# A decode kernel's first load, 128 rows of wq, issued as sixteen rows and then 112, with the load behind it issued after the framework's barrier

## The chip, the cores and the metric

The kernel runs on one core of a Trainium2 chip. The metric is the device time of one execution in microseconds (us). The times of the kernel before are three runs: median 1362.75, from 1362.43 to 1364.05.

## The reference

One token goes through a block with attention over a cache and a gated feed-forward part, side by side, all in float32:

```python
xn = _layernorm(x)                                    # x: 1 x 1 x 576
q = (xn @ wq).reshape(B, Sq, H, Dh)                   # wq: 576 x 4096, 32 heads of 128
scores = einsum("bhqd,bhkd->bhqk", q, k_cache) * Dh ** -0.5   # k_cache: 32 heads x 16384 x 128
o = einsum("bhqk,bhkd->bhqd", softmax(scores), v_cache)       # v_cache: as k_cache
h = gelu(xn @ w_gate) * (xn @ w_up)                   # 576 x 4608 each
return x + o @ wo + h @ w_down                        # wo: 4096 x 576, w_down: 4608 x 576
```

The two caches are 268 MB each; all that the kernel has to read is 587.6 MB.

## The kernel before, in words

The program is written out by hand as one list of operations for each engine (class `Plan`). `Plan.op` and `Plan.dma` append to an engine's list with the semaphore counts that it has to wait for; `Plan.ahead` issues the first operations of a list before the framework's barrier, and `Plan.run` emits the rest behind it, in the block at L128. Nothing reorders the lists.

All large loads go out from SyncE (SP), in the order of its list, so they stand one behind the other in one DMA queue, which 16 DMA engines work off. Each load of 128 rows is 128 packets of one row each where a row is up to 64 KB (the cache's rows of 64 KB are one packet, and those of wq's first load are 32 KB). The order is:

- wq in three loads: `qw[0]` (128 partitions, 32 KB each, the first and second of four row groups), `qt` (the 64 tail rows of wq, laid on 128 partitions, 8 KB each), `qw[1]` (as `qw[0]`, the third and fourth row group);
- w_gate, and behind VectorE's work on wq w_up, in the same three parts;
- K and V of the heads in turn, 8.4 MB each, in a loop, each behind the release of its buffer (`s_kf` after VectorE's sums, `s_vf` after TensorE's use of V);
- w_down in two parts and wo in many, at the end.

The projections of the token are made on VectorE: `rows` multiplies the first row group by its part of the token (L264), adds the second (L253), then the tail's, then the third and fourth. Its first product waits for the load `qw[0]`, its third step for `qt`, its fourth for `qw[1]`. TensorE sums over the partitions behind it. In the loop VectorE makes K times q (L356) and the sums (L360); TensorE makes the product with V (L344). At the end VectorE adds the products of w_down and of a part of wo to `wacc` (L253), TensorE those of the rest of wo (L478), and 2.3 KB are written.

`Plan.ahead` is called with two operations of SP and one of ACT: the loads `qw[0]` and `qt` on SP and the token's row `xrow` on ACT stand before the barrier; all else is behind it.

Of the kernel before, what the change touches and what calls it, by code (L numbers as in the profile page):

```python
# [13 lines left out]
P = 128  # L14
# [8 lines left out]
HD = H * DH  # L23
# [9 lines left out]
SIDE = 160  # L33
LEFT = 2 * SIDE
ASIDE = 8
SEL = 396


class Plan:
# [14 lines left out]
    def op(self, e, fn, *deps, sig=None, by=1):  # L54
        if e in ("dve", "act", "pool"):
            deps += (self.last.get(e),)
        sig = sig or self.own[e]
        self.count[sig.name] = self.count.get(sig.name, 0) + by
        self.q[e].append((deps, fn, sig, by))
        if sig is self.own[e]:  # L60
            self.last[e] = sig, self.count[sig.name]
        return sig, self.count[sig.name]

    def dma(self, e, out, in_, *deps, sem=None):
        sem = sem or self.sem(f"d{len(self.count)}")
        return self.op(e, lambda g: g.dma_start(out, in_), *deps, sig=sem, by=16)
# [55 lines left out]
@with_exitstack  # L122
def kernel(ctx: ExitStack, tc: tile.TileContext, x, k_cache, v_cache, wq, wo, wg, wu, wd, out):
    pl = Plan(tc)
    last, done = plan(tc.nc, pl, x, k_cache, v_cache, wq, wo, wg, wu, wd, out)
    pl.ahead({"sp": 2, "act": 1})
    tc.close()
    tc.compile()  # L128
    pl.run(last, done)


def plan(nc, pl, x, k_cache, v_cache, wq, wo, wg, wu, wd, out):
    op, dma = pl.op, pl.dma
# [10 lines left out]
    def small(name, shape, where=None):  # L144
        if where is None:
            size = 4
            for n in shape[1:]:
                size *= n
            where = place[name] = top[0]
            top[0] += -(-size // 32) * 32  # L150
            assert top[0] <= S0, (name, top)
        return nc.alloc_sbuf_tensor_at(name, shape, F32, offset=where).ap()

    def big(name, floats, where):
        assert where + 4 * floats <= 3 * SLOT
        return nc.alloc_sbuf_tensor_at(name, [P, floats], F32, offset=S0 + where).ap()
# [14 lines left out]
    gu, hT = small("gu", [P, 2, FT]), small("hT", [P, FT])  # L171
    sel = small("tmp", [P, 3 * SEL])
    over = place["tmp"]
# [7 lines left out]
    qw, qt = [big("q0", 2 * HD, C + 8 * HD), big("q2", 2 * HD, C)], big("qt", HD // 2, C - 2 * HD)  # L181
    both = big("both", 12 * SEL, C + 8 * DF + 256)
    gw, gt = [big("g0", 2 * DF, B + 10240), big("g2", 2 * DF, A - 4 * DF)], big("gt", DF // 2, B)
# [21 lines left out]

    main = {n: w[:DM].rearrange("(p j) f -> p (j f)", j=DJ) for n, w in (("q", wq), ("g", wg), ("u", wu))}
    tail = {n: w[DM:].rearrange("d (s f) -> (d s) f", s=2) for n, w in (("q", wq), ("g", wg), ("u", wu))}
    d_q = [dma("sp", qw[0], main["q"][:, : 2 * HD]), dma("sp", qt, tail["q"]), dma("sp", qw[1], main["q"][:, 2 * HD :])]
    d_x = dma("act", xrow, xf)
    d_g = [dma("sp", gw[0], main["g"][:, : 2 * DF]), dma("sp", gt, tail["g"]), dma("sp", gw[1], main["g"][:, 2 * DF :])]  # L210

# [49 lines left out]
    def rows(w, t, d, parts, between=None):  # L261
        n = w[0].shape[-1] // 2
        r = [u[:, j * n : (j + 1) * n] for u in w for j in range(2)]
        op("dve", lambda g: g.tensor_scalar(r[0], r[0], xp[:, :1], None, op0=ALU.mult), d[0], k_x)  # L264
        add(r[1], r[1], xp[:, 1:2], r[0])
        made = between and between()
        for i in range(2):
            c = r[1][:, i * n // 2 : (i + 1) * n // 2]
            add(c, t, xt[:, i : i + 1], c, d[1])
        k_s = add(r[2], r[2], xp[:, 2:3], r[1], d[2])  # L270
        v = [u.rearrange("p (i c) -> p i c", i=4) for u in (r[3], r[2])]
        for lo, hi, to in parts:
            k = add(bv[:, :, to : to + hi - lo], v[0][:, :, lo:hi], xp[:, 3:4], v[1][:, :, lo:hi])
        pads = [op("pool", lambda g, lo=lo, hi=hi: g.memset(bv[:, :, lo:hi], 0.0), k_s)
                for lo, hi in ((384, SEL), (SEL + 384, 2 * SEL), (2 * SEL + 256, 3 * SEL)) if len(parts) > 1]
        pl.then("dve", [s_r], k, *pads[-1:])
        return k_s, k, made

    def sums(g):
        with g.Fori(0, 3):  # L280
# [3 lines left out]
            for b in range(3):  # L284
                for i in range(4):
                    m = g.matmul(pw[32 * i : 32 * i + 32, b, :SEL], ones[:, :32], bv[:, i, b * SEL : (b + 1) * SEL], start=True, stop=True)  # L286
            m.then_inc(s_w, 1)
# [3 lines left out]
    def select(dst, c, r, n):  # L291

        t = dst.shape[-1]
        v = sel[:, : 3 * c].rearrange("p (b r t) -> p b r t", b=3, t=t)
        m = m32[:, : 3 * c // t].rearrange("p (b r) -> p b r", b=3).unsqueeze(3).to_broadcast([P, 3, c // t, t])
        k = op("dve", lambda g: g.tensor_mul(v, pw[:, :, :c].rearrange("p b (r t) -> p b r t", t=t), m), (s_w, n), c_m32)
        return op("dve", lambda g: g.tensor_reduce(dst, sel[:, : r * t].rearrange("p (r t) -> p t r", r=r), axis=AX.X, op=ALU.add), k)  # L297

    _, q_k, _ = rows(qw, qt, d_q, [(384 * b, min(384 * b + 384, HD // 4), SEL * b) for b in range(3)])
    d_u = [dma("sp", uw[0], main["u"][:, : 2 * DF], q_k), dma("sp", ut, tail["u"]), dma("sp", uw[1], main["u"][:, 2 * DF :])]  # L300
# [8 lines left out]

    u_k, _, k_g = rows(uw, ut, d_u, [(0, DF // 4, 0)], lambda: select(gu[:, 0], SEL, 32, 2))  # L310

# [132 lines left out]
    for n in WO_CUTS:  # L444
        w, base, dep = (wo0, 0, (s_kf, 2)) if lo < WO1 else (wo1, WO1, k_w0)
        c = w[:, (lo - base) * D : (lo - base + n) * D]
        d = dma("sp", c, wov[:, lo * D : (lo + n) * D], dep)
# [22 lines left out]
    for t in ON_DVE:  # L470
        for i, c in enumerate((oT[: P // 2, WT - 1 :], o31) if t == ASIDE else ()):
            to = o_sum[: P // 2, LEFT:]
# [19 lines left out]
    for i, t in enumerate(rows):  # L492
        w, d = d_wo[t]
        k = whole(32 * (i % 4), oT[:, t : t + 1], w, (d, k_oT), i < 4, i >= len(rows) - 4)
    k_part = op("dve", lambda g: g.tensor_tensor(part, acc[:, :, :HALF], wacc, op=ALU.add), k, k_w1)  # L495
    for t in range(WT - LAST, WT - 2):
        w, d = d_wo[t]
# [14 lines left out]
    d = dma("sp", of, to, c, c0, c1)  # L512
# [28 lines left out]
```

## Time and profile before

| what | before |
|---|---|
| median of three runs | 1362.75 us (1362.43 to 1364.05) |
| profiled execution: span, first to last instruction | 1360.5 us |
| profiled execution: its own time, taken as the median | 1362.75 us, 2.25 us around the span |
| DMA: data read in the span, mean rate | 587.60 MB, 432 GB/s |
| DMA engines busy with the hardware queue of SP and ACT | 99.8% |
| VectorE (DVE) busy | 1243.5 us, 91% |
| TensorE (PE) busy | 391.3 us, 29% |

No time is listed for the profiled execution beside its span, so its own time is taken as the span and what lies around it. The span of 1360.5 us lies 2.25 us below the median of the three runs, and that difference stands for what lies ahead of the first instruction and behind the last one. In the tables by window, the DMA share is the packet time of the 16 DMA engines in the stretch, and a packet is counted whole in the stretch where it starts: so a short stretch in which 16 packets start can show a share over 1, and one in which none starts shows 0 although all engines are busy. Share times length is then the mean time of a packet, when 16 start in the stretch.

### The profile page before, as it was taken

To read this page: it belongs to the slowest core of one execution; us is meant where nothing else is said; L and a number is where in the kernel's file an instruction comes from. 1 tells how busy PE (TensorE), PEld (TensorE's weight loads), DVE (VectorE), ACT (ScalarE), POOL (GpSimd) and SP (SyncE) were. 2 spreads that over 40 slices of the span, in tenths; PEclk is the share of its full clock that TensorE was granted. 3 is DMA by queue.
4 is the path that set the end of the run, shared out by engine and by line. 5 is a ranking of instruction groups with operands and counts; after the bars stand their busy time and mean duration, and the time that the engine had idled before them with its cause. 6 is when DMAs were issued, how large, how long until landed. Compare 5 with 4: busy or idle time off the path is not lost. (4 is left out here: it accounts for less than half of the span.)

```text
span 1360.5 us, 6992 instructions
## 1 busy us (share of the span) xinstructions
PE 391.3 (29%) x2650; PEld 122.4 (9%) x2650; DVE 1243.5 (91%) x228; ACT 66.9 (5%) x234; POOL 36.0 (3%) x25
## 2 busy tenths in 40 slices
PE   0211233333211333333222333332223333322136
PEld 0000011001000111100000111010001111000011
DVE  7999999999988888898888888998888889988888
ACT  0000000000000000000000000000000000000000
POOL 0063000000000000000000000000000000000000
PEclk9655666666556666666556666655666666655667
DMA  9999999999999999999999999999999999999998
GB/s 405 429 437 432 434 447 441 432 432 432 434 432 434 432 432 432 435 451 435 432 432 432 434 432 434 432 432 432 441 447 434 432 432 434 432 434 432 431 432 374
DMA packets 12870, 587.63 MB, mean 432 GB/s; under 512 B 1474, under 2 KB 1986, under 8 KB 2756
## 3 DMA queue, kind: packets, MB, share of 16 engines
q1 hardware_dynamic: 12866, 587.60, 99.8%
q8 instruction: 1, 0.02, 0.0%
q10 hardware_dynamic: 2, 0.00, 0.0%
q14 instruction: 1, 0.01, 0.0%
HBM read 587.60 MB, written 0.00 MB: 432 GB/s over the span
## 5 line engine op out<-in xcount | busy, mean ns | idle before, releaser
L344 PE MATMUL po<-vt,pe 128*4 128x512 f32 x2048 | 291.8, 733 | 611.5 <-PEq L119 611.5
L356 DVE TENSOR_TENSOR kb<-kb,qb 128x16384 f32<-128x16384 f32 (+1 forms) x17 | 277.3, 16314 | 31.8 <-DVEq L119 31.8
L356 DVE TENSOR_TENSOR ka<-ka,qb 128x16384 f32<-128x16384 f32 x16 | 275.6, 17226 | 32.1 <-DVEq L119 32.1
L360 DVE TENSOR_REDUCE sc<-kb 128x128 f32<-128x16384 f32 x16 | 275.5, 17220 | 2.3
L360 DVE TENSOR_REDUCE sc<-ka 128x128 f32<-128x16384 f32 x16 | 275.5, 17220 | 2.3
L344 PEld LDWEIGHTS po<-vt,pe 128*4 128x4 f32 x2048 | 56.3, 98 | 819.9 <-issue 819.9
L337 PE MATMUL pt<-ident,pm 128*1 128x128 f32 x32 | 11.9, 372 | 223.1 <-PEq L119 223.1
L397 ACT ACTIVATE o<-po 128x512 f32<-128x512 f32 x32 | 19.1, 597 | 877.1 <-ACTq L119 877.1
L349 PE MATMUL pc<-m,o 128*128 128x1 f32 x256 | 32.7, 249 | 28.9 <-PEq L119 28.9
L349 PEld LDWEIGHTS pc<-m,o 128*128 128x128 f32 x256 | 31.0, 191 | 57.8 <-issue 57.8
L253 DVE SCALAR_TENSOR_TENSOR wacc<-wd,hT,wacc 128x576 f32<-128x576 f32 x36 | 29.5, 819 | 4.1 <-DMA wd<-in_B_w_down_dram 2.9
L286 PE MATMUL pw<-both,ones 128*32 128x396 f32 x72 | 11.5, 801 | 63.3 <-PEq L119 63.3
L365 DVE TENSOR_REDUCE nm<-pt 1x1 f32<-1x128 f32 x32 | 8.9, 278 | 21.5 <-DVEq L119 21.5
L337 PEld LDWEIGHTS pt<-ident,pm 128*1 128x1 f32 x32 | 2.5, 79 | 228.2 <-issue 228.2
L339 PE MATMUL pb<-nm,ones 1*128 1x1 f32 x64 | 17.7, 343 | 18.5 <-PEq L119 18.5
L339 PEld LDWEIGHTS pb<-nm,ones 1*128 1x128 f32 x64 | 15.9, 307 | 27.8 <-issue 27.8
L393 ACT ACTIVATE nb<-pb 128x1 f32<-128x1 f32 x32 | 5.5, 171 | 254.1 <-ACTq L119 254.1
L363 DVE TENSOR_REDUCE pm<-sc 128x1 f32<-128x128 f32 x32 | 9.2, 286 | 7.6 <-DVEq L119 7.6
L335 PE MATMUL pqb<-qsel,hsel 128*128 128x128 f32 x64 | 14.9, 315 | 1.8 <-PEq L119 1.8
L395 ACT ACTIVATE pe<-sc,nb 128x128 f32<-128x128 f32 x32 | 12.8, 401 | 6.1 <-ACTq L119 6.1
L304 ACT ACTIVATE hsel<-hcol 128x128 f32 (+1 forms) x34 | 10.2, 301 | 41.3 <-DVE qsel L297 41.2
L326 POOL TENSOR_TENSOR tmp<-tmp 128x576 f32<-128x576 f32 (+3 forms) x4 | 11.3, 2836 | 0.3
(93 smaller groups left out, 177.9 us busy)
## 6 DMA issues: line engine op xcount, KB each, us to landing
g<-in_B_w_gate_dram SPq DMA_DIRECT2D x2, 4608.0 KB, 39.5
u<-in_B_w_up_dram SPq DMA_DIRECT2D x2, 4608.0 KB, 32.3
q<-in_A_wq_dram SPq DMA_DIRECT2D x2, 4096.0 KB, 17.4
kb<-in_A_k_cache_dram SPq DMA_DIRECT2D x2, 4096.0 KB, 26.7
wd<-in_B_w_down_dram SPq DMA_DIRECT2D x1, 8064.0 KB, 42.0
wo<-in_A_wo_dram SPq DMA_DIRECT2D x1, 3456.0 KB, 35.9
wo<-in_A_wo_dram SPq DMA_DIRECT2D x2, 1728.0 KB, 28.6
wd<-in_B_w_down_dram SPq DMA_DIRECT2D x1, 2304.0 KB, 28.1
```

What stands on the lines that cost most here:

```text
L253: return op("dve", lambda g: g.scalar_tensor_tensor(out, w, c, into, op0=ALU.mult, op1=ALU.add), *deps)
L286: m = g.matmul(pw[32 * i : 32 * i + 32, b, :SEL], ones[:, :32], bv[:, i, b * SEL : (b + 1) * SEL], start=True, stop=True)
L326: k = op("pool", lambda g, o=o, r=r: g.tensor_tensor(o, v[:, :r, :], v[:, r : 2 * r, :], op=ALU.add), k)
L335: g.matmul(pqb[:, 0, :DH], hsel, qsel, start=True, stop=True).then_inc(s_pq, 1)
L337: g.transpose(pt[:1, 0, :P], pm, ident).then_inc(s_pt, 1)
L339: g.matmul(pb[:, 0, :1], ones[:1, :], nm, start=True, stop=True).then_inc(s_pb, 1)
L344: m = g.matmul(po[q : q + 4, 0, :], pe[:, k : k + 4], vt[:, k * DH : (k + 4) * DH], start=k < 16, stop=k >= N - 16)
L349: m = g.matmul(pc[:, 0, :1], o4[:, j * DH : (j + 1) * DH], m32[:, j : j + 1], start=j == 0, stop=j == 3)
L356: g.tensor_mul(kd, kd, qb[i].unsqueeze(1).to_broadcast([P, n[1] - n[0], DH])).then_inc(s_d, 1)
L360: g.tensor_reduce(sc[i], kt[i].rearrange("p (n d) -> p n d", d=DH), axis=AX.X, op=ALU.add).then_inc(s_d, 1)
L395: g.activation(pe, sc[i], AF.Exp, bias=nb, scale=SCALE, accum_out=ls[:, bass.ds(h, 1)]).then_inc(s_p, 1)
L397: g.activation(o4, po[:, 0, :], AF.Copy).then_inc(s_o4, 1)
```

## The change

The load of `qw[0]` is made as two loads: partitions 0 to 15, and partitions 16 to 127. Both count up one semaphore, `wq`, by 16 each, and VectorE's first product waits for its value 32, that is for both. `Plan.ahead` still takes two operations of SP, which are now these two; the load `qt` stands behind the barrier, ahead of `qw[1]`.

```diff
+FIRST = 16
...
-    d_q = [dma("sp", qw[0], main["q"][:, : 2 * HD]), dma("sp", qt, tail["q"]), dma("sp", qw[1], main["q"][:, 2 * HD :])]
+    s_q = pl.sem("wq")
+    for a, b in ((0, FIRST), (FIRST, P)):
+        d = dma("sp", qw[0][a:b], main["q"][a:b, : 2 * HD], sem=s_q)
+    d_q = [d, dma("sp", qt, tail["q"]), dma("sp", qw[1], main["q"][:, 2 * HD :])]
```

SP's list at the start of the program before. `q_98` is `qw[0]`, `q_99` is `qw[1]`, `g_102` and `gt` are parts of w_gate; the branch at L128 is the entry of the block, the wait ahead of L113 is the barrier.

```order
0 L536 UNCONDITIONAL_BRANCH [waits barrier_Pool_Activation_PE_DVE_SP_release]
1 L66 DMA q_98<-in_A_wq_dram 128x8192
2 L66 DMA qt<-in_A_wq_dram 128x2048
3 L128 UNCONDITIONAL_BRANCH
4 L113 UNCONDITIONAL_BRANCH [waits barrier_Pool_Activation_PE_DVE_SP_release]
5 L66 DMA q_99<-in_A_wq_dram 128x8192
6 L66 DMA g_102<-in_B_w_gate_dram 128x9216
```

The same place in the changed program, whose lines stand one to four lower in the file:

```order
0 L540 UNCONDITIONAL_BRANCH [waits barrier_Pool_Activation_PE_DVE_SP_release]
1 L67 DMA q_98<-in_A_wq_dram 16x8192
2 L67 DMA q_98<-in_A_wq_dram 112x8192
3 L129 UNCONDITIONAL_BRANCH
4 L114 UNCONDITIONAL_BRANCH [waits barrier_Pool_Activation_PE_DVE_SP_release]
5 L67 DMA qt<-in_A_wq_dram 128x2048
6 L67 DMA q_99<-in_A_wq_dram 128x8192
7 L67 DMA g_102<-in_B_w_gate_dram 128x9216
```

The one row of 128 partitions has become two, `qt` has moved from ahead of the barrier to behind it, and everything after it stands one place later. The order in which the bytes stand in the DMA queue is the same.

VectorE's list around its first products before; `d0`, `d1` and `d2` are the semaphores of the three loads of wq:

```order
21 L243 MEMSET fin 128x512 [waits c_dve]
22 L264 TENSOR_SCALAR q_98<-q_98,xp 128x4096 [waits c_dve,d0]
23 L253 SCALAR_TENSOR_TENSOR q_98<-q_98,xp 128x4096 [waits c_dve]
24 L253 SCALAR_TENSOR_TENSOR q_98<-qt,xt,q_98 128x2048 [waits c_dve,d1]
25 L253 SCALAR_TENSOR_TENSOR q_98<-qt,xt,q_98 128x2048 [waits c_dve]
26 L253 SCALAR_TENSOR_TENSOR q_99<-q_99,xp,q_98 128x4096 [waits c_dve,d2]
```

And in the changed program:

```order
21 L247 MEMSET fin 128x512 [waits c_dve]
22 L268 TENSOR_SCALAR q_98<-q_98,xp 128x4096 [waits c_dve,wq]
23 L257 SCALAR_TENSOR_TENSOR q_98<-q_98,xp 128x4096 [waits c_dve]
24 L257 SCALAR_TENSOR_TENSOR q_98<-qt,xt,q_98 128x2048 [waits c_dve,d1]
25 L257 SCALAR_TENSOR_TENSOR q_98<-qt,xt,q_98 128x2048 [waits c_dve]
26 L257 SCALAR_TENSOR_TENSOR q_99<-q_99,xp,q_98 128x4096 [waits c_dve,d2]
```

Nothing moves on VectorE: the first product waits for the shared semaphore in place of `d0`.

## The prediction

> **What bounds the kernel now.** I read the page first, for the shares of the whole span.
>
> ```profile
> span 1360.5 us, 6992 instructions
> ...
> PE 391.3 (29%) x2650; PEld 122.4 (9%) x2650; DVE 1243.5 (91%) x228; ACT 66.9 (5%) x234; POOL 36.0 (3%) x25
> ...
> q1 hardware_dynamic: 12866, 587.60, 99.8%
> ...
> HBM read 587.60 MB, written 0.00 MB: 432 GB/s over the span
> ```
>
> The queue that carries all loads keeps the 16 DMA engines busy for 99.8% of the span. VectorE comes next with 91%. So the question for any edit is whether a DMA engine stands still, or moves bytes more slowly, for longer or shorter than before.
>
> Then the table by windows, for the start (quarters of a microsecond and whole waves of packets) and for the middle. The columns are busy time of PE, PEld, DVE, ACT and POOL, the granted clock, the DMA share and the rate.
>
> ```profile
> 1.25:1.50 0.25, 0.00 (x0) 0.00 (x0) 0.00 (x0) 0.00 (x0) 0.00 (x0) 1.00 0.00 0
> 1.50:1.75 0.25, 0.00 (x0) 0.00 (x0) 0.00 (x0) 0.00 (x0) 0.00 (x0) 1.00 0.10 9
> 1.75:2.00 0.25, 0.00 (x0) 0.00 (x0) 0.00 (x0) 0.00 (x0) 0.00 (x0) 1.00 5.32 1442
> 2.00:2.25 0.25, 0.00 (x0) 0.00 (x0) 0.00 (x0) 0.00 (x0) 0.00 (x0) 1.00 1.79 524
> 2.25:2.50 0.25, 0.00 (x0) 0.00 (x0) 0.00 (x1) 0.10 (x1) 0.10 (x1) 1.00 0.42 131
> ```
>
> ```profile
> 1.50:2.75 1.25, 0.00 (x0) 0.00 (x0) 0.19 (x2) 0.35 (x1) 0.20 (x1) 1.00 1.53 421
> ...
> 7.00:8.25 1.25, 1.18 (x6) 0.87 (x6) 0.61 (x4) 0.00 (x0) 0.00 (x0) 1.00 0.97 419
> 8.25:9.25 1.00, 0.00 (x0) 0.00 (x0) 0.54 (x2) 0.00 (x0) 0.00 (x0) 1.00 1.21 524
> ```
>
> ```profile
> 100.00:1300.00 1200.00, 349.88 (x2361) 107.89 (x2365) 1103.86 (x126) 57.91 (x213) 13.83 (x9) 0.62 1.00 434
> ```
>
> Nothing moves before 1.50 us. Then comes the token's row (9 GB/s in 0.25 us is 2.3 KB), and from 1.75 us the first sixteen 32 KB packets of wq: 1442, 524 and 131 GB/s in quarters are 11, 4 and 1 of them. Sixteen packets start in 1.50 to 2.75 us, and share times length gives their mean time: 1.53 x 1.25 = 1.91 us. Later waves take 1.21 x 1.00 = 1.21 us: 32,768 bytes in 1.21 us is 27 GB/s for an engine, and sixteen of them make the 434 GB/s of the middle with a share of 1.00. The engines are at one steady rate from the second wave on.
>
> Last the waits, the issues and the chain, for the question whether a shift at the start reaches the end.
>
> ```profile
> DVE ka L356 <- DVEq L119: 32.1, 13, 2.6
> DVE kb L356 <- DVEq L119: 31.8, 16, 2.6
> ```
>
> ```profile
> vt<-in_A_v_cache_dram SPq DMA_DIRECT2D x32, 28.0
> ...
> ka<-in_A_k_cache_dram SPq DMA_DIRECT2D x16, 42.1
> kb<-in_A_k_cache_dram SPq DMA_DIRECT2D x15, 42.0
> ```
>
> ```profile
> 1308.09 28.10 DMA wd<-in_B_w_down_dram
> 1336.19 0.02 issue
> 1336.21 0.83 DVE wacc L253
> ```
>
> A cache load of 8.4 MB needs 8.4 / 0.434 = 19.3 us, but lands 28 or 42 us after its issue: it stands 9 us or more behind others in the queue. VectorE waits some 2 us for each K ((32.1 + 31.8) / 29). The chain that ends last comes out of a DMA, the second part of w_down. So all that the queue loses at the start is there at the end, one for one, and all that it gains too.
>
> **The change part by part.** The sum is made on the span of 1360.5 us; the median of 1362.75 lies 2.25 above it, and I add the difference to the median. About 0.2%, 2.7 us, is what a measurement of this kernel can tell from no change.
>
> ```profile
> 0.73 0.41 SPq L66 DMA_DIRECT2D q<-in_A_wq_dram  x1
> 0.74 0.51 ACTq L66 DMA_DIRECT2D xrow<-in_A_x_dram  x1
> 1.21 0.40 SPq L66 DMA_DIRECT2D qt<-in_A_wq_dram  x1
> ...
> 2.39 0.33 SPq L66 DMA_DIRECT2D q<-in_A_wq_dram  x1
> ```
>
> *An earlier first packet.* The one-row load of ACT is issued at 0.74 and moves from the quarter at 1.50; the 128-row load is issued at 0.73 and moves from the quarter at 1.75, its last engine from that at 2.25. A load of sixteen rows lies between them. At most its sixteen packets all start with the token's row, 0.5 us sooner for the middle ones; at least nothing changes. I take -0.2 us, since fifteen of sixteen already start within 0.5 us.
>
> *The load qt behind the barrier.* It is issued at about 2.4 instead of 1.21, and each load behind it 0.4 us later, one issue's time. The queue reaches qt only when eight waves are through, at about 1.75 + 1.91 + 7 x 1.21 = 12.1 us. The cover is 9.7 us; if it went, the cost would be what is missing of it. Nothing.
>
> *The second load's issue.* The 112 rows are issued at 1.21 and needed when the first packets end, at 1.75 + 1.91 = 3.66 at the earliest. If the issue takes longer than 0.40, the barrier opens later:
>
> ```profile
> 1309.41 5.89 SPq L66 DMA_DIRECT2D aside<-in_A_wo_dram  x8
> ...
> 12.98 2.35 DVE L264 TENSOR_SCALAR q<-q,xp 128x4096 f32<-128x4096 f32 x1 [2.15 <-DMA q<-in_A_wq_dram]
> ```
>
> The loads of eight rows cost 5.89 / 8 = 0.74 us each, so at worst 0.34 us more. VectorE, ACT and POOL wait behind the barrier, but VectorE then idles 2.15 us for wq. Nothing.
>
> *One load more.* It has one more completion for each engine, of a few bytes. The sum of the middle (share 1.00 with a load each 19 us) leaves no room for more than some hundredths of a microsecond. Nothing.
>
> *The narrow first load.* This is the term that decides. In the load of 128 rows each engine has eight packets, 128 / 16, and they run at 27 GB/s side by side; no load of many neighbouring partitions stands in this trace. I ask what sets 1.21 us: the engine itself, or the way into the eight partitions that it fills. If it is the engine, sixteen rows run as now. If it is the way, sixteen neighbouring partitions reach, at eight partitions a way, from two ways (blocks of eight) to sixteen (dealt out singly). Two ways take 8 x 1.21 = 9.7 us, sixteen take 1.21. The middle by factors is between four and eight ways; I take four, since blocks of eight are the simpler deal of the two ends: 4 x 1.21 = 4.84 us, against 1.91 us for the first wave before. All engines are held by it, since each has one row of the sixteen and the second load stands behind it: 4.84 - 1.91 = +2.93 us. The start-up of 0.70 us (1.91 - 1.21) I take as lying within the 4.84; the bound is +0.70 more.
>
> [...]
>
> *The 112 rows.* Four ways have had half of their eight rows; twelve ways still have all eight, 8 x 1.21 = 9.68 us, where an engine has only seven, 8.47. So at least +1.21 if the ways bind. Neighbouring engines now take seven neighbouring rows each, which cross from one way to the next at uneven places, so two engines meet at a way while another is free. I take one packet's time for the last engine, +1.21; the ends are 0 and three packets, 3.63, if an engine is held up at each of the two or three ways that seven rows cross. Behind it the loads have 128 rows again and no engine catches up, since the queue never runs dry.
>
> Sum: -0.2 + 2.93 + 1.21 + 1.21 = +5.15, so 1362.75 + 5.15 = 1367.9 us. The ends of this case are -0.5 + 2.93 = +2.4, nothing in the second load, and -0.2 + 2.93 + 0.70 + 1.21 + 3.63 = +8.3; most of it lies in 1365.3 to 1370.5.
>
> **The rivals.**
>
> *The engines set the rate, not the ways.* Then sixteen rows run side by side like any other wave and only the earlier start is left: 0 to -0.5, at -0.2 us 1362.55. For it speaks that the steady 1.21 us looks the same on every engine, which an engine's own rate explains as well. It decides between slower and not slower: as soon as the two loads lose less than 2.7 us together, the result can't be told from no change. Eight ways belong here too: 2 x 1.21 - 1.91 + 1.21 = +1.7, 1364.5. Chance 0.27, most of it for no sharing at all.
>
> *Rows are dealt to engines by their partition, not by count.* Then the sixteen rows fall to the few engines that fill these partitions anyway, four rows each, and the other engines start with the second load, issued 1.21 - 0.73 = 0.48 us later. Each engine still has eight rows in all, and the end moves by about +0.5: 1363.2. For it speaks that the load of 128 rows goes without any engine in another's way. Against it, the loads of eight rows are issued at another price than those of 128, as if the number of rows sets the split. Chance 0.09.
>
> *Two ways or worse.* The first load takes 9.7 us or the 112 rows block each other at every step: 9.7 - 1.91 + 1.21 = +9.0 and more, 1371.8 upward. Chance 0.04.
>
> **How the numbers follow.** The forecast, 1367.9, has the chance 0.60. Of it some 0.02 lies below +2.7 us; with the last rival that makes 0.62 slower. Within 0.2% lie the first two rivals and that 0.02, 0.38 less 0.01 for a gain that I can't derive, 0.37. Faster by over 0.2% has 0.01: the head start has no more than 1.75 us of empty queue to give. The range has to reach to the first rival, or more than 2 in 10 is left out: 1362.3 (1362.55 less the spread of the runs) to 1370.5, above which lie the last rival and the top of the forecast's case. The likeliest case's own range is 1365.3 to 1370.5.
>
> **What the profile after would show.** If the forecast holds, the windows at the start show sixteen packets with a mean time near 4.8 us instead of 1.91, an empty rate until about 6.5 us, and packets of wq well over 1.21 us up to about 17 us; VectorE's first product starts at about 16 to 18 us instead of 12.98; from there on all rows are shifted, with 434 GB/s in the middle. If the ways don't bind, the first packets still take some 1.9 us and VectorE starts at 12.8 to 13.0. If rows are dealt by partition, few packets start at 1.75 us and the others half a microsecond later. The prediction is wrong if VectorE's first product starts late and the end doesn't move, which would mean that the queue has slack somewhere, or if the middle runs at another rate than 434 GB/s.

## The result: 8.6 us slower, lost in the first load alone

The changed kernel takes 1371.3 us (median of four runs, 1370.39 to 1371.86), the kernel before 1362.74 us. The ratio is 1.0063, with a 95% interval from 1.0048 to 1.0077: slower by 8.6 us. The forecast was slower, 1367.9 us, with a range up to 1370.5: the side was right, and so was the cause as far as the experiments measure it: which partitions a load names sets how long its packets take (1372.85 us with two loads of 64 neighbouring partitions, 1362.8 us with the even and the odd ones). A way, the prediction's word for a path into a group of partitions, is the author's picture behind it; the runs show the times of packets. The size was not right.

The page of the changed kernel, with the span, the rates by slice and the queue's share:

```profile
span 1369.5 us, 6993 instructions
...
GB/s 293 431 448 429 429 431 448 431 435 431 429 433 448 431 433 431 429 448 433 435 429 431 431 448 431 435 431 429 436 444 433 431 431 429 450 431 435 428 427 375
...
q1 hardware_dynamic: 12882, 587.60, 99.8%
```

And the rates by slice of the kernel before:

```profile
GB/s 405 429 437 432 434 447 441 432 432 432 434 432 434 432 432 432 435 451 435 432 432 432 434 432 434 432 432 432 441 447 434 432 432 434 432 434 432 431 432 374
```

The same bytes in 16 packets more, and the same 99.8%: by their busy time the DMA engines are as full as before. Only the first slice of 34 us is slow, with 293 GB/s where before had 405. Over the first 34 us the DMA share is 0.96 in both kernels, at 293 and 406 GB/s (window 0 to 34): the same busy share went with two rates.

The table by windows of the changed kernel: the sixteen packets of the narrow load (1.50 to 3.00), the 112 of the second (5.00 to 20.00), the middle. The last two columns are the DMA share and the rate. In any window the mean time of a 32 KB packet is 524 KB (sixteen of them) x share / rate.

```profile
1.50:3.00 1.50, 0.00 (x0) 0.00 (x0) 0.28 (x3) 0.61 (x1) 0.37 (x2) 1.00 2.53 351
5.00:20.00 15.00, 1.47 (x7) 1.16 (x7) 3.97 (x12) 0.29 (x1) 0.00 (x0) 1.00 1.01 245
100.00:1300.00 1200.00, 347.22 (x2339) 107.70 (x2331) 1104.21 (x127) 59.89 (x217) 18.46 (x9) 0.62 1.00 435
```

And the seven later waves of the first load in the kernel before:

```profile
3.50:12.00 8.50, 1.47 (x7) 1.16 (x7) 5.28 (x16) 0.48 (x2) 0.17 (x1) 1.00 1.00 432
```

A packet of the narrow load takes 524 x 2.53 / 351 = 3.78 us, where the first wave of before took 1.91. A packet of the 112 rows takes 524 x 1.01 / 245 = 2.16 us, before 1.21. An engine has one of the first and seven of the second: (3.78 - 1.91) + 7 x (2.16 - 1.21) = 1.87 + 6.65 = 8.5 us, which is the loss. In the middle the rate is 435 GB/s, as before (434).

The seven waves (sixteen packets each) of the 112 rows aren't alike. The first of them, right behind the narrow load:

```profile
5.00:6.50 1.50, 0.00 (x0) 0.00 (x0) 1.07 (x4) 0.29 (x1) 0.00 (x0) 1.00 1.90 350
```

It takes 524 x 1.90 / 350 = 2.85 us a packet. The six others, by the same formula, take between 1.81 us (10.25 to 11.50) and 2.22 us (16.00 to 17.50). No single packet of the 112 in the trace took less than 1.63 us.

VectorE's first product in the timeline, and a row of the DMA issues (us from issue to landing at the end):

```profile
22.68 2.35 DVE L268 TENSOR_SCALAR q<-q,xp 128x4096 f32<-128x4096 f32 x1 [11.86 <-DMA q<-in_A_wq_dram]
```

```profile
ka<-in_A_k_cache_dram SPq DMA_DIRECT2D x16, 42.1
```

The product starts 9.7 us later than at 12.98, and the span is 9.0 us longer (1369.5 against 1360.5). The cache loads land as long after their issue as before (42.1 us for these): what stands behind the first load is shifted.

### The profile page after: what moved, and what is told of

The parts are those of the page before. It is cut to its first block, busy times and chain, and to the rows that moved or that the text cites. A ratio compares the mean times of both kernels' runs of the same rounds, so it can differ in the third digit from the quotient of the medians.

```text
span 1369.5 us, 6993 instructions
## 1 busy us (share of the span) xinstructions
PE 392.1 (29%) x2650; PEld 122.7 (9%) x2650; DVE 1243.5 (91%) x228; ACT 66.9 (5%) x234; POOL 35.4 (3%) x25
## 3 DMA queue, kind: packets, MB, share of 16 engines
q1 hardware_dynamic: 12882, 587.60, 99.8%
## 5 line engine op out<-in xcount | busy, mean ns | idle before, releaser
L341 PE MATMUL pt<-ident,pm 128*1 128x128 f32 x32 | 11.9, 371 | 226.1 <-PEq L120 226.1
L268 DVE TENSOR_SCALAR q<-q,xp 128x4096 f32<-128x4096 f32 x1 | 2.4, 2354 | 11.9 <-DMA q<-in_A_wq_dram 11.9
```

The source lines that it names most:

```text
L341: g.transpose(pt[:1, 0, :P], pm, ident).then_inc(s_pt, 1)
```

## The experiments

Each kernel was compared with the kernel before in the same batch of runs (its median there was 1362.55 us for the first four, 1362.42 for the four of the second batch and 1362.35 for the last).

**Which part of the change.** First the move of `qt` behind the barrier without the split:

```diff
-    pl.ahead({"sp": 2, "act": 1})
+    pl.ahead({"sp": 1, "act": 1})
```

> The load of 128 rows is whole as before; only qt moves behind the barrier. If the loss comes from the narrow loads (theory: the partitions that a load names set how many ways into them its packets have), this is the time before, 1362.7 us within 0.5, and VectorE's first product starts at 12.9 to 13.0 us. If the move of qt were the cause, it would be at 1371.

Measured: 1362.42 us, ratio 1.0001 (0.9991 to 1.001). The move costs nothing. Then the split without the move:

```diff
 # the changed kernel, with
-    pl.ahead({"sp": 2, "act": 1})
+    pl.ahead({"sp": 3, "act": 1})
```

> The split into sixteen rows and 112 alone, with qt ahead of the barrier as before (three loads ahead of it). Theory of the ways: all of the loss is here, 1371.3 us within 0.7, first product at about 22.7 us. If the move of qt takes part, it is less, down to 1362.7.

Measured: 1371.27 us, ratio 1.0064 (1.0048 to 1.0081). All of the loss is in the split.

**Two loads, or which partitions they name.** Two loads again, with the shared semaphore, but each with all partitions:

```diff
-    for a, b in ((0, FIRST), (FIRST, P)):
-        d = dma("sp", qw[0][a:b], main["q"][a:b, : 2 * HD], sem=s_q)
+    for a, b in ((0, HD), (HD, 2 * HD)):
+        d = dma("sp", qw[0][:, a:b], main["q"][:, a:b], sem=s_q)
```

> The first load is two loads that share a semaphore, as in the change, but split by columns: each has all 128 partitions and half of the bytes of a row. Theory of the ways: no loss, 1362.7 us within 0.5. Rival, that two loads for one, the shared semaphore or the smaller packets cost: 1364 to 1371.

Measured: 1362.36 us, ratio 0.9997 (0.9987 to 1.0007). One load more, the semaphore and packets of half the size cost nothing that can be told. Then 64 rows and 64:

```diff
-FIRST = 16
+FIRST = 64
```

> The split at 64 in place of 16, so that each load has 64 neighbouring rows, four for each engine. Theory of the ways with four ways to sixteen neighbours: if 64 neighbours reach eight ways, each load takes 8 x 1.21 = 9.7 us in place of 4.85, so +9 us and 1372; if 64 neighbours reach all sixteen, no loss, 1362.7. Rival, that the loss comes from loads with few rows or with an odd number of rows for each engine (seven): 1362.7 to 1363.5.

Measured: 1372.85 us, ratio 1.0077 (1.0061 to 1.0094), +10.3 us: worse than sixteen and 112, so few rows are not the cause. And 64 and 64 once more, but even and odd:

```diff
-    for a, b in ((0, FIRST), (FIRST, P)):
-        d = dma("sp", qw[0][a:b], main["q"][a:b, : 2 * HD], sem=s_q)
+    for i in range(2):
+        d = dma("sp", qw[0][i::2], main["q"][i::2, : 2 * HD], sem=s_q)
```

> The first load is split into the even and the odd partitions, 64 rows each. Theory of the ways: the even partitions reach all sixteen ways (the probe of 64 rows at every second partition had 1.21 us a packet), so nothing is lost, 1362.6 us within 0.5. Rival, that a load of 64 rows in place of 128 costs whatever partitions it names: 1372.9, as the split into two halves of neighbouring rows.

Measured: 1362.8 us, ratio 1.0003 (0.9993 to 1.0012). The same number of loads, rows and bytes as in the halves, and 10 us between them. The window over the seven later waves, of the halves and of the even and odd partitions:

```profile
4.00:22.00 18.00, 1.47 (x7) 1.16 (x7) 5.39 (x16) 0.59 (x2) 0.22 (x2) 1.00 0.99 205
```

```profile
3.50:12.50 9.00, 1.47 (x7) 1.16 (x7) 5.62 (x17) 1.08 (x2) 0.65 (x3) 1.00 0.95 409
```

A packet takes 524 x 0.99 / 205 = 2.53 us with neighbouring halves and 524 x 0.95 / 409 = 1.22 us with every second partition. So it is the partitions named in each load that make the loss.

**Loads by themselves.** The first probe puts twelve loads ahead of the kernel, one at a time; all of SP's loads stand behind the barrier in both probes. A row of its list is a name, the partitions written and the rows read:

```diff
+    p = None
+    for n, to, src in (
+        ("low16", lambda t: t[0:16], main["q"][0:16, : 2 * HD]),
+        ("by7", lambda t: t[0:106:7], main["q"][0:16, : 2 * HD]),
+        ("top112", lambda t: t[16:128], main["q"][16:128, : 2 * HD]),
...
+    ):
+        p = dma("sp", to(big(n, 2 * HD, A + 6 * DF)), src, p)
```

> Twelve extra loads into an unused place ahead of the kernel, one at a time, each issued when the one before has landed; all rows are 32 KB. They are not part of the computation, and the time of the whole is not compared. Theory of the ways (four neighbouring partitions to a way, sixteen ways, so that 32 rows further on a way comes again): beyond a fixed part f of 2 to 3 us, all 128 rows take 9.7 us, low16 4.85, by7 (sixteen rows at partitions 0, 7, ..., 105) 1.2 to 2.4, by8 2.4, low32 4.85, low64 9.7, by2 (64 rows at every second partition) 4.85 to 9.7, top112 9.7 to 15, top96 9.7. Rival, that only the number of rows and their deal to the engines counts: low16, by7 and by8 alike at 1.2, low64 and by2 alike at 4.85, top112 and low112 8.5. Rival, that the source addresses in HBM set it: low16, by7 and by8 alike whatever their time, since they read the same rows.

The windows of sixteen rows at partitions 0 to 15, at every seventh and at every eighth partition, and of the 112 rows:

```profile
27.00:31.50 4.50, 0.00 (x0) 0.00 (x0) 0.00 (x0) 0.00 (x0) 0.00 (x0) 1.00 0.82 117
34.10:36.80 2.70, 0.00 (x0) 0.00 (x0) 0.00 (x0) 0.00 (x0) 0.00 (x0) 1.00 0.77 194
38.60:41.70 3.10, 0.00 (x0) 0.00 (x0) 0.00 (x0) 0.00 (x0) 0.00 (x0) 1.00 0.75 169
```

```profile
71.00:86.00 15.00, 0.00 (x0) 0.00 (x0) 0.00 (x0) 0.00 (x0) 0.00 (x0) 1.00 0.94 245
```

By the same formula a packet of the three forms takes 3.67, 2.08 and 2.33 us, start-up included. They read the same sixteen rows, so the source in HBM is not what sets it, and neither is the number of rows: the partitions written are. The 112 rows take 2.01 us a packet with nothing ahead of them. One expectation was clearly missed: 96 rows at 32 to 127, expected at 9.7 us, took 2.36 us a packet (share 0.95, rate 211 from 103.60 to 118.50), 14.2 us for an engine's six, and landed 16.5 us after their issue.

The second probe sends several loads of one form back to back, so that the steady packet shows; its list has a count of repeats beside each form:

```diff
+        ("foursix", lambda t: t[0:61:4], main["q"][0:16, : 2 * HD], 6),
...
+    ):
+        p = [dma("sp", to(big(n + str(j), 2 * HD, 8 * HD * j)), r, *p) for j in range(reps)]
```

> A second probe ahead of the kernel, whose time isn't compared: extra loads of 32 KB rows into unused places (not part of the computation), several of one form back to back so that the steady time of a packet shows. Theory, a way for four neighbouring partitions that comes again 32 or 64 partitions on: sixteen rows at 0 to 15 run at 4 x 1.21 = 4.85 us a packet, at every fourth partition 1.21 (if a way comes again after 64) or 2.42 (after 32), at every seventh 1.21 to 2.42, at every eighth 2.42; 32 neighbouring rows 2.42, at every second partition 2.42, at every fourth 1.21 to 2.42; 64 neighbouring rows at 32 to 95 between 1.21 and 2.42, at every second partition 1.21; 96 and 112 rows 1.8 to 2.5. Rival, that the number of rows alone counts: all forms with the same number alike.

The windows, in this order: sixteen rows at 0 to 15; at every fourth, seventh and eighth partition; 32 rows at 0 to 31, at every second and at every fourth partition; 64 rows at 32 to 95 and at every second partition; 96 rows at 0 to 95; 112 rows at 0 to 111. The last two hold the start-up of their load, the others leave the first wave out:

```profile
18.50:42.80 24.30, 0.00 (x0) 0.00 (x0) 0.00 (x0) 0.00 (x0) 0.00 (x0) 1.00 0.95 102
49.00:61.70 12.70, 0.00 (x0) 0.00 (x0) 0.00 (x0) 0.00 (x0) 0.00 (x0) 1.00 0.91 186
66.60:78.90 12.30, 0.00 (x0) 0.00 (x0) 0.00 (x0) 0.00 (x0) 0.00 (x0) 1.00 0.93 197
84.00:96.80 12.80, 0.00 (x0) 0.00 (x0) 0.00 (x0) 0.00 (x0) 0.00 (x0) 1.00 0.91 184
101.50:114.20 12.70, 0.00 (x0) 0.00 (x0) 0.00 (x0) 0.00 (x0) 0.00 (x0) 1.00 0.94 191
119.30:132.00 12.70, 0.00 (x0) 0.00 (x0) 0.00 (x0) 0.00 (x0) 0.00 (x0) 1.00 0.95 194
136.40:142.50 6.10, 0.00 (x0) 0.00 (x0) 0.00 (x0) 0.00 (x0) 0.00 (x0) 1.00 1.00 430
146.80:155.70 8.90, 0.00 (x0) 0.00 (x0) 0.00 (x0) 0.00 (x0) 0.00 (x0) 1.00 0.91 394
159.30:168.10 8.80, 0.00 (x0) 0.00 (x0) 0.00 (x0) 0.00 (x0) 0.00 (x0) 1.00 0.97 417
169.40:184.30 14.90, 0.00 (x0) 0.00 (x0) 0.00 (x0) 0.00 (x0) 0.00 (x0) 1.00 0.96 211
186.00:200.80 14.80, 0.00 (x0) 0.00 (x0) 0.00 (x0) 0.00 (x0) 0.00 (x0) 1.00 0.95 248
```

| rows | partitions | us a packet |
|---|---|---|
| 16 | 0 to 15 | 4.88 |
| 16 | every fourth, to 60 | 2.57 |
| 16 | every seventh, to 105 | 2.47 |
| 16 | every eighth, to 120 | 2.59 |
| 32 | 0 to 31 | 2.58 |
| 32 | every second, to 62 | 2.57 |
| 32 | every fourth, to 124 | 1.22 |
| 64 | 32 to 95 | 1.21 |
| 64 | every second, to 126 | 1.22 |
| 96 | 0 to 95 | 2.39 |
| 112 | 0 to 111 | 2.01 |

Sixteen neighbours take four times 1.21 (4.88 against 4.84), as on four ways. Sixteen rows spread over 0 to 60 and 32 rows at 0 to 31 take about twice 1.21 (2.57 and 2.58 against 2.42), as on eight. 32 rows spread over 0 to 124 take 1.22, as on all. And 64 neighbours run at 1.21 from 32 on, while from 0 on they took 524 x 0.77 / 157 = 2.57 us in the first probe (53.50 to 61.20), as 32 neighbours from 0 on did: partitions 32 to 63 add nothing to 0 to 31, and partitions from 64 on add to 32 to 63. This fits a way that comes again 32 partitions further. Four rows to a way is an estimate: 16 x 1.21 / 4.88 = 4.0 ways for sixteen neighbours. No probe has fewer rows, and no run shows a way itself. The rival, that the number of rows counts, has no place left: 16 rows take 4.88 or 2.47, 32 rows 2.58 or 1.22.

The table says more. The 96 rows at 0 to 95 and the 112 at 0 to 111 hold the partitions 32 to 95, whose 64 rows alone ran at 1.21, and took 2.39 and 2.01. So the number of ways that a load reaches, by this reading, doesn't give its rate by itself. The sixteen rows seven apart, though six of them lie at 70 or above, took 2.47, hardly less than the 2.57 of sixteen rows at 0 to 60. What sets this pace isn't shown: all forms of sixteen rows read the same rows over and over, and none of them ran faster than 2.47.

**The two terms apart.** The parts in the other order:

```diff
-    for a, b in ((0, FIRST), (FIRST, P)):
+    for a, b in ((FIRST, P), (0, FIRST)):
```

> The change with the two parts of the first load in the other order, 112 rows first. Theory: the two terms add up in any order, 14.96 us for the 112 rows alone (the probe) and 4 x 1.21 for the sixteen, 19.8 in place of 10.75: +9, 1371.3 to 1371.8. Rival, that the 112 rows are slow because the sixteen ahead of them have put the engines out of step: clearly less, 1365 to 1368.

Measured: 1371.65 us, ratio 1.0070 (1.0054 to 1.0087), +9.2 us, as the sum of the two. The 112 rows are slow by themselves (2.01 us a packet with nothing ahead of them in the first probe), not because the sixteen put the engines out of step. Then sixteen extra rows, not needed by the computation, ahead of the whole load:

```diff
+    s_q = pl.sem("wq")
+    dma("sp", big("extra", 2 * HD, A + 4 * DF)[0:16], main["q"][:16, : 2 * HD], sem=s_q)
-    d_q = [dma("sp", qw[0], main["q"][:, : 2 * HD]), ...
+    d_q = [dma("sp", qw[0], main["q"][:, : 2 * HD], sem=s_q), ...
```

> The whole first load of 128 rows, with sixteen rows more ahead of it, to partitions 0 to 15 of an unused place (0.5 MB that the computation doesn't need). It measures the first term by itself. Theory: 3.79 us for the packets of the narrow load in place of 1.88 for the first wave, and one wave more, +1.9 + 1.2: 1365.7 us. If the sixteen rows cost only their bytes: 1363.8. If they put all that follows out of step: 1368 and more.

Measured: 1366.28 us, ratio 1.0028 (1.0016 to 1.0039), +3.86 us, 1.21 of it for the bytes: the narrow load costs 2.65 us, more than the 1.9 expected. Its own packets take 524 x 2.45 / 351 = 3.66 us (1.50 to 3.00), 1.75 more than the first wave before. The rest falls on the wave behind it:

```profile
4.50:6.50 2.00, 0.00 (x0) 0.00 (x0) 1.53 (x5) 0.29 (x1) 0.00 (x0) 1.00 1.20 262
```

That wave takes 524 x 1.20 / 262 = 2.40 us in place of 1.21, though it belongs to a load of 128 rows; the next is at 1.21 again (7.50 to 8.50). By the packets that makes 1.75 + 1.19 = 2.9 us. And with `[0:106:7]` in place of `[0:16]`:

> The same sixteen extra rows, read from the same addresses, to partitions 0, 7, ..., 105. Theory of the ways: little more than their bytes, +1.2 and about 0.2 for the longer first packets (2.06 us in place of 1.88): 1364.0 us. Rival, that few rows are what costs: 1365.7, as with neighbouring partitions.

Measured: 1364.43 us, ratio 1.0016 (1.0006 to 1.0026), +2.0 us, of which 1.21 are bytes. Spread over the partitions the same rows cost 1.9 us less. The rest of 0.8 is more than the 0.2 expected. The issue of this form takes 0.66 us in place of 0.41, and its first packets start in 2.00 to 2.50 us, a good quarter of a microsecond later; the wave behind them takes 524 x 1.21 / 350 = 1.81 us (3.80 to 5.30), 0.6 more than 1.21.

**The rule used the other way round.** If the table holds, it gives the time of a split that was never made:

```diff
-    for a, b in ((0, FIRST), (FIRST, P)):
+    for a, b in ((32, 96), (0, 32), (96, P)):
```

> The first load in three parts of neighbouring partitions: 32 to 95, then 0 to 31, then 96 to 127, all ahead of the barrier. By the second probe's packets, 64 rows at 32 to 95 run at 1.21 us a packet (four for each engine), 32 neighbours from 0 at 2.56 (two for each engine), and 32 neighbours from 96 the same: (2 + 2) x (2.56 - 1.21) = +5.4 us, 1367.9. If an engine that is done with its rows at 0 to 31 fills free ways at 96 to 127, less: 1365 to 1367. Rival, that any 64 rows cost what the halves cost: 1372 and more.

Measured: 1367.74 us, ratio 1.0040 (1.0026 to 1.0054), +5.4 us: the total as worked out. The windows over the 64 middle rows and over the two parts of 32:

```profile
2.00:7.00 5.00, 0.00 (x0) 0.00 (x0) 2.59 (x11) 1.58 (x2) 0.91 (x4) 1.00 1.09 419
7.00:16.00 9.00, 1.47 (x7) 1.17 (x7) 3.29 (x9) 0.00 (x0) 0.00 (x0) 1.00 1.05 233
```

The middle packets take 524 x 1.09 / 419 = 1.36 us with the start-up wave among them, about as much as before ((1.91 + 3 x 1.21) / 4 = 1.39), so this part loses nothing. The others take 2.36, not the 2.56 that the expectation used: 4 x (2.36 - 1.21) = 4.6 us of the 5.4. The first packets start a quarter of a microsecond later (none before 2.00 us), and the other half microsecond isn't accounted for; that the total fits to a tenth is in part luck. No split that was run beats the kernel before beyond the interval.

## Why the prediction was right in kind and wrong in size

- *What bounds the kernel, and that a shift at the start reaches the end.* Right. The first load's loss of 8.5 us is the loss of the whole; the middle runs at the same rate and the cache loads land as long after their issue.
- *An earlier first packet, -0.2 us.* Wrong, and small. It isn't there: in the changed kernel 9 packets start in the quarter from 1.75 us (1180 GB/s x 0.25 us / 32.8 KB), before 11. The load of sixteen rows didn't start sooner than the one of 128.
- *The move of qt, the second issue, one load more: nothing.* Right (the move alone 1362.42 us; two loads by columns 1362.36).
- *The narrow first load, four ways, +2.93 us.* Right in its factor: 4.88 us a packet is four times 1.21 where such loads follow one another. As a term it was somewhat large: the first packets took 3.78 and not 4.84 us, which makes 1.87, and 2.65 with the extra load, where the slow wave behind it is counted too. The start-up did lie within it.
- *The 112 rows, 1.21 + 1.21 us.* This is the step that failed. They cost 6.65 us, more than the 4.84 of its upper end. The prediction counted the rows that each way holds and, where two engines meet at a way, let the last engine lose one packet's time, or three at most. In the trace all seven waves are slow, 2.16 us a packet in the mean, and 2.01 with nothing ahead of them. No run shows the two terms of 1.21, or two engines that meet at a way; what the runs show in their place is that all sixteen engines were slow, and not only the last: the fastest of the 112 packets took 1.63 us. Some of the 6.65, in the wave at 2.85 us, is owed to the narrow load ahead. With 7 x (2.16 - 1.21) in place of +2.42, without the -0.2 and with 1.87 for the narrow load, the sum is 1362.75 + 8.5 = 1371.3; this takes its terms from the run that it explains, so it is an account and not a test.
- *The range.* Its top of 1370.5 hung on that term too; the case's own end of +8.3 was left outside the range, and the result, +8.6, lies just past that end too.
- *The rivals.* That the engines set the rate fell with the halves against the even and odd partitions. That rows are dealt by their partition fell as well: then an engine's packets would keep their 1.21 us, and they took 3.78 and 2.16. Two ways or worse, at 0.04, has in its second half, that the 112 rows block each other at every step, what comes nearest to the runs, and its 1371.8 lies 0.5 us from the result. But that price was made from a first load of 9.7 us, whose packets took 3.78, so the nearness is luck.
- *The signs in the profile.* The middle's rate held. The first packets took 3.78 us and not 4.8, the next ones started from 5.0 us on and not at 6.5, and VectorE's first product came at 22.68 us and not at 16 to 18.

What stays open is why 112 rows take 2.01 to 2.16 us a packet and 96 rows 2.39, though they hold the partitions 32 to 95 that alone run at 1.21. If two of the sixteen packets in flight met at a way all the time, and all the others went at their pace, a packet would take about 2 x 1.21 = 2.42 us, as an estimate. The 96 rows are near that, the 112 below it. But no row shows which engine has which row, and the prediction's seven neighbours to each engine are shown by none either, so this is argued and not shown.

## What to carry to other kernels

In this kernel a load that covers 128 partitions ran at 1.21 us a packet from its second wave on, and so did 32 rows at every fourth partition (1.22), 64 at every second (1.22) and 64 at 32 to 95 (1.21). To hold such partitions wasn't enough: 96 and 112 neighbours hold 32 to 95 too and took 2.39 and 2.01. Cut at 16 or at 64, a split by neighbouring partitions made both parts slow, the large one too (3.78 and 2.16 us a packet, and 2.53 for the halves). If the first load has to be cut, cut its columns or take every second partition: here these took 1362.36 and 1362.8 us, no more than the kernel before that can be told. The busy share of the DMA engines, 99.8% before and after, doesn't show this loss: look at the time of a packet, which is bytes of a wave times share over rate.

## What the runs showed of the hardware that was not expected

- Sixteen rows seven apart, spread over the partitions 0 to 105, took 2.47 us a packet, a little over the upper end of the 1.21 to 2.42 that was expected. And the narrow load slowed the wave of the load behind it, 2.40 us in place of 1.21 (the kernel with the extra rows).
- The forms at about twice the steady packet lie somewhat above it: 2.57 us (every fourth partition to 60, every second to 62) against 2 x 1.21 = 2.42. The form at four times lies hardly above it: 4.88 against 4.84.
- A load of 96 neighbouring rows took longer than one of 128, 16.6 us against 11.9. In the second probe, from issue to landing (the last column):

```profile
again<-in_A_wq_dram SPq DMA_DIRECT2D x1, 4096.0 KB, 11.9
...
lowninety<-in_A_wq_dram SPq DMA_DIRECT2D x1, 3072.0 KB, 16.6
```

- How long an issue took wasn't set by the number of rows alone: 0.41 us for sixteen neighbouring rows (the kernel with the extra rows) and for 128 of them in the kernel before, 0.66 for sixteen rows seven apart. Nor did neighbouring rows make it short by themselves: the two issues of the halves, 64 neighbours each, took 1.23 us together, those of sixteen and 112 rows 0.86.
